# First four attention groups by 64x64 matmuls, the first q and k turned in fp32, 1e-9 as a 65th column, and the issue order of all engines from a table

## The chip, the cores and the metric

The kernel runs on one NeuronCore of one Trainium2 chip. The core has five instruction streams that run side by side and wait for one another by semaphores: TensorE (PE in the profile; its weight loads are a row of their own, PEld), VectorE (DVE), ScalarE (ACT), GpSimd (POOL) and SyncE (SP). Transfers between HBM and the core's memory are issued by POOL, SP and ACT; those of POOL cost POOL time to write their descriptors. Every stream works strictly in the order in which its instructions were written, so an instruction that waits holds up all that stand behind it on its engine.

The metric is the device time of one execution in microseconds (us), as the median of several runs. A lower number is better.

## The reference

```python
def reference(q, k, v, moe_w_in, moe_w_out):          # q, k, v: [8, 8, 576, 64] fp32
    # attention inside chunks of 64 tokens, for each of 8 batches and 8 heads
    q_c, k_c, v_c = (t.reshape(8, 8, 9, 64, 64) for t in (q, k, v))
    scores = (1 / 8) * q_c @ k_c.transpose(0, 1, 2, 4, 3)
    scores = scores - scores.max(-1, keepdims=True)
    attn = exp(scores)
    attn = attn / (attn.sum(-1, keepdims=True) + 1e-09)
    x = (attn @ v_c) -> [4608 tokens, 512]
    h = x @ moe_w_in                                   # [512, 2048]
    g = maximum(0.01 * h, h)
    return g @ moe_w_out                               # [2048, 512] -> [4608, 512] fp32
```

## The kernel before

**Tiling.** The 4608 tokens are 36 groups `u` of 128 tokens (two chunks of 64), and four groups make one of nine blocks `j` of 512 tokens. Attention is done by group. The two linear layers are done by block: block 0 and 1 do the first layer by plain matmuls with a moving side of 128 columns (tasks `L1.j.h.a.p`: block, group within the block, and which 256 columns of `w_in`), the other blocks by seven products in place of eight (`Q1`..`Q7`), and the second layer of all blocks is done by seven products (`P1`..`P7`). PE computes in fp16.

**One attention group** is a chain of tasks; the number behind the dot is the group:

- `loadq`, `loadk`: POOL fetches q and k of the group, fp32 in HBM, fp16 in SBUF. Group 0 comes instead by `q_f` and `k_f` on the queues of SP and ACT, without a conversion, and is cast by `castq`, `castk0`, `castk1`.
- `tq`, `tk`: four PE transposes each (128x128) into PSUM, for groups 0 to 11; for the others a DMA does it.
- `q0`, `q1`: the turned q is copied by ACT or DVE into a tile QZ that is half zeros, each chunk of 64 tokens to its own half of the columns, so that one 128-row matmul computes one head of both chunks. `k`: the same for k in one copy.
- `s`: eight matmuls 128x64 give the scores. `m`, `b`, `x`, `z`: row maximum (DVE), subtraction (DVE), exponential (ACT, fp16 out), row sum (DVE).
- `ze`, `zi`, `n`: add 1e-9 to the sums (DVE or POOL), reciprocal (DVE), scale (DVE or POOL).
- `e`, `c`: PE turns the weights, ACT or DVE copies them; from group 20 a DMA does this instead.
- `v`: eight matmuls with v, 128x64 each, against a tile that has v in two quarters and zeros in the others. `a`: ACT copies the result to xT, the input of the first layer.

For groups 0 to 3 the rows of v come by `v_f` and `loadw`, four copies `put0`..`put3` for each group spread them over a tile (buffers S1 and S2) that four DVE memsets `zg` have zeroed. Later groups use tiles VB that `loadv` fills directly and `zv` has zeroed.

```python
nc.tensor.matmul(                                     # s, before: 8 of these
    out=t["sp"][:, i, :], lhsT=mem(qz)[:, 2 * m + g, e, :, :], rhs=mem(kt)[:, 2 * m + g, e, :],
    start=(i == 0), stop=True, skip_group_check=True)
...
nc.tensor.matmul(                                     # v, before: 8 of these
    out=t["xp"][:, i, e, :], lhsT=vg(u)[:, i, e] if u in VROW else VB[b % NVB][:, i, c, :],
    rhs=mem(et)[:, i // 2, e, i % 2, :], start=(e == 0 and i == 0), stop=True, skip_group_check=True)
```

**Order.** The order of work is not written out. Each piece is a task with an engine (or a choice of engines), an estimated duration, dependencies and the buffers that it holds; `Plan.run` plays them through with its own model of durations and transfers, picks on each engine the ready task with the lowest key, and emits the instructions in the order of the planned starts. The keys are shifted by some 1400 numbers (`NUDGE`) and 36 tasks are moved by hand afterwards (`MOVES`). Where the plan has PE idle in the first 24 us, it puts in matmuls whose result nobody reads (`idle`, 140 in all), after 45 of the same kind at the very start (`warm`).

POOL's loads are bound in one more way: eight transfers may be under way, so a ninth waits for the landing of the one eight places ahead of it. The lines that the profile names for these tasks: L1995 `warm`, L2677 `idle`, L2143 `tq` and `tk`, L2212 `s`, L2218 `m`, L2221 `b`, L2225 `x`, L2237 `z`, L2240 `ze`, L2243 `zi`, L2246 `n`, L2272 `e`, L2290 `v`, L2370 `L1`, L2421 the `Q` products, L2543 the `P` products, L2007 and L2009 all copies on ACT and DVE, L1925 `loadq` and `loadk`, L1940 the loads of `w_in`, L1937 `loadv`, L1986 `ident`.

Of the kernel before, what the change touches and what calls it, by code (L numbers as in the profile page):

```python
# [15 lines left out]
LATENCY = {PE: 0.2, ACT: 0.15, DVE: 0.18, POOL: 0.2, SP: 0.2}  # L16


class Buf:


    def __init__(self, ring):
        self.ring, self.slot, self.open, self.since, self.till = ring, None, 0, 0.0, 0.0


class Task:
    def __init__(self, name, engs, key, emit, deps, bufs, opens, after, bank):
        self.name, self.engs, self.key, self.emit = name, engs, key, emit
        self.eng = next(iter(engs))
        self.deps, self.bufs, self.opens, self.after, self.bank = deps, bufs, opens, after, bank  # L30
        self.next, self.start, self.end, self.seen = [], None, None, None

    @property
    def us(self):
        return self.engs[self.eng]


class Dma:


    LAG = {"soft": 1.7, "hard": 0.5}
    SHARE = {"soft": 0.38, "hard": 0.62}
    SPARE = {"soft": 0.0, "hard": 0.0}

    def __init__(self):
        self.rings = {"soft": [], "hard": []}
        self.now = 0.0
        self.known = None
        self.wide = False

    def add(self, ring, at, work, t):
# [2660 lines left out]
```

## Time and profile before

| | |
|---|---|
| median of 3 runs | 279.45 us (278.21 to 279.82) |
| profiled execution, first to last instruction (span) | 276.6 us |
| what lies around the span, median less span | 2.8 us |
| PE busy | 267.6 us, 97% of the span |
| DVE, ACT, POOL busy | 226.7, 207.9, 139.1 us |

The profile gives one execution, so a sum of its durations is compared with its span, and the 2.8 us around it are taken to stay as they are. PE's busy time counts the unread matmuls `warm` and `idle` as well. Matmuls are pipelined: the one with 128 columns is listed with 219 ns, but eight in a row start some 56 ns apart.

### The profile page before, as it was taken

Reading aid. Unit: us, or ns where it says so; the run is one execution under the profiler, and the core shown is the slowest. Engines: PE = TensorE matmul, PEld = TensorE weight load, DVE = VectorE, ACT = ScalarE, POOL = GpSimd, SP = SyncE. Lnnn points to the kernel's source line nnn. Section 1 sums busy time; section 2 is a strip of 40 time slices with the busy share of each in tenths; the row PEclk is TensorE's granted clock in tenths of the full one; section 3 lists DMA queues with packets and bytes.
Section 4 is the critical chain, followed back from the end, with each engine's and each line's share of the span. In section 5 each row is a group of like instructions: output and inputs, shape, how many; then the busy total and the mean of one; then the engine's idle time right before and its main releaser. Section 6 shows DMA issues by size and latency. Waiting matters only on the chain.

```text
span 276.6 us, 8050 instructions
## 1 busy us (share of the span) xinstructions
PE 267.6 (97%) x3257; PEld 242.9 (88%) x3257; DVE 226.7 (82%) x426; ACT 207.9 (75%) x396; POOL 139.1 (50%) x180
## 2 busy tenths in 40 slices
PE   7888999999999999999999999999999999999995
PEld 7777999999988979898989889889899888988884
DVE  6888899899989899899998999888699927734942
ACT  6878999786786899799877897476877767677431
POOL 8978688567776338244936996562333120000000
PEclk9999999999999999999999999999999999999999
DMA  9999999999999989999999999999543032200132
GB/s 148 162 178 173 166 176 194 139 154 114 149 186 169 190 103 123 113 168 194 136 179 143 154 169 168 211 142 213 113 94 118 19 40 81 76 2 0 68 146 92
DMA packets 157237, 37.09 MB, mean 134 GB/s; under 512 B 147601, under 2 KB 152849, under 8 KB 157201
## 3 DMA queue, kind: packets, MB, share of 16 engines
q0 software_dynamic: 113904, 17.96, 100.9%
q1 hardware_dynamic: 42256, 18.36, 37.7%
q8 instruction: 25, 0.41, 0.7%
q10 hardware_dynamic: 1040, 0.26, 0.4%
q14 instruction: 12, 0.09, 0.1%
HBM read 36.70 MB, written 9.44 MB: 167 GB/s over the span
## 4 chain that ended last, share of the span: by engine, by line
PE 81%; DMA 9%; POOL 5%; ACT 1%; DVE 1%; issue 1%; POOLq 0%
PE bank L2543 38%; PE bank L2421 30%; PE bank L2370 6%; DMA VB<-in_v_dram 4%; DMA w_inT<-in_moe_w_in_dram 3%; PE bank L2290 3%; PE bank L2212 2%; DMA qk<-in_k_dram 2%; POOL qk L1925 2%; PE bank L2272 1%; POOL xs L2093 1%; PE bank L2143 1%; PE bank L2585 1%; DVE xs L2317 1%; ACT ex L2225 0%
## 5 line engine op out<-in xcount | busy, mean ns | idle before, releaser
L2347 ACT ACTIVATE gT<-bank 128x512 f16<-128x512 f32 x116 | 64.9, 600 | 13.9 <-PE bank L2421 12.3
L2543 PEld LDWEIGHTS <-gT 128*128 128x128 f16 x576 | 55.2, 98 | 6.3
L2543 PE MATMUL bank<-w_outT,gT 128*128 128x256 f16 x432 | 53.7, 273 | 0.0
L2421 PEld LDWEIGHTS <-FI 128*128 128x128 f16 x448 | 43.2, 98 | 5.7 <-issue 0.9
L2421 PE MATMUL bank<-xs,FI 128*128 128x256 f16 x336 | 45.8, 272 | 0.4 <-ACT bank L2007 0.3
L2543 PEld LDWEIGHTS <-S 128*128 128x128 f16 x416 | 39.7, 98 | 4.7 <-DVE S L2489 0.3
L1925 POOL DMA_DIRECT2D qk<-in_q_dram x39 | 33.8, 870 | 10.9 <-DMA QT<-qk 4.2
L1925 POOL DMA_DIRECT2D qk<-in_k_dram x39 | 34.0, 878 | 8.6 <-DMA KT<-qk 5.6
L2421 PEld LDWEIGHTS <-w_inT 128*128 128x128 f16 x336 | 32.1, 98 | 3.9 <-issue 0.2
L2543 PE MATMUL bank<-FO,S 128*128 128x256 f16 x280 | 34.8, 273 | 0.0
L2370 PE MATMUL bank<-xT,w_inT 128*128 128x128 f16 x512 | 32.7, 219 | 0.3 <-DMA w_inT<-in_moe_w_in_dram 0.3
L2421 PE MATMUL bank<-xT,w_inT 128*128 128x256 f16 x224 | 31.6, 273 | 0.0
L2370 PEld LDWEIGHTS <-w_inT 128*128 128x128 f16 x512 | 29.4, 98 | 0.5 <-DMA w_inT<-in_moe_w_in_dram 0.5
L2007 ACT ACTIVATE p<-bank 128x512 f32<-128x512 f32 (+1 forms) x37 | 20.6, 588 | 10.0 <-PE bank L2543 5.7
L2246 POOL TENSOR_TENSOR en<-ex,z 128x512 f16<-128x512 f16 x18 | 20.6, 1149 | 14.0 <-DVE z L2243 5.3
L2237 DVE TENSOR_REDUCE z<-ex 128x8 f32<-128x512 f16 x36 | 24.4, 677 | 2.7 <-ACT ex L2225 2.4
L2218 DVE TENSOR_REDUCE mx<-bank 128x8 f32<-128x512 f32 x36 | 24.5, 682 | 1.8 <-PE bank L2212 1.5
L2446 DVE TENSOR_TENSOR bank<-bank,p 128x512 f32<-128x512 f32 x28 | 19.0, 694 | 8.3 <-PE bank L2421 5.9
L2225 ACT ACTIVATE ex<-sh 128x512 f16<-128x512 f32 x35 | 22.2, 634 | 3.0 <-DVE sh L2221 1.5
L2221 DVE TENSOR_TENSOR sh<-bank,mx 128x512 f32<-128x512 f32 x35 | 23.7, 680 | 0.5
L2240 POOL TENSOR_SCALAR z<-z 128x8 f32<-128x8 f32 x25 | 7.5, 301 | 32.7 <-DVE z L2237 26.7
L2007 ACT ACTIVATE xT<-bank 128x512 f16<-128x512 f32 x36 | 21.2, 599 | 3.0 <-PE bank L2290 2.8
(84 smaller groups left out, 479.2 us busy)
## 6 DMA issues: line engine op xcount, KB each, us to landing
out_dram<-osb SPq DMA_DIRECT2D x16, 512.0 KB, 5.2
VB<-in_v_dram POOLq DMA_DIRECT2D x14, 288.0 KB, 7.8
qk<-in_k_dram POOLq DMA_DIRECT2D x31, 128.0 KB, 6.5
qk<-in_q_dram POOLq DMA_DIRECT2D x31, 128.0 KB, 7.9
w_outT<-in_moe_w_out_dram POOLq DMA_DIRECT2D x4, 512.0 KB, 11.0
w_inT<-in_moe_w_in_dram POOLq DMA_DIRECT2D x6, 256.0 KB, 6.9
qk<-in_k_dram POOLq DMA_DIRECT2D x8, 64.0 KB, 7.0
w_inT<-in_moe_w_in_dram POOLq DMA_DIRECT2D x4, 128.0 KB, 6.3
```

Source lines behind the costliest of these rows:

```text
L1925: nc.gpsimd.dma_start(out=to[a - r0:z - r0, which], in_=src[a // S, :, a % S:a % S + z - a, :].rearrange("h p d -> p h d"),)
L2007: nc.scalar.activation(out=to(), in_=of(), func=AFT.Copy, bias=0.0, scale=1.0)
L2218: nc.vector.tensor_reduce(out=mem(mx)[:, 0], in_=t["sp"], axis=AXL.X, op=ALU.max)
L2221: nc.vector.tensor_tensor(out=mem(sh), in0=t["sp"], in1=mem(mx)[:, 0].unsqueeze(2).to_broadcast((128, 8, CH)), op=ALU.subtract)
L2225: nc.scalar.activation(out=mem(ex), in_=mem(sh), func=AFT.Exp, bias=0.0, scale=SCL)
L2237: nc.vector.tensor_reduce(out=mem(z)[:, 0], in_=mem(ex), axis=AXL.X, op=ALU.add)
L2246: (nc.gpsimd if eng == POOL else nc.vector).tensor_tensor(out=mem(en), in0=mem(ex), in1=mem(z)[:, 2].unsqueeze(2).to_broadcast((128, 8, CH ...
L2347: nc.scalar.activation(out=to, in_=of, func=AFT.Prelu, bias=0.0, scale=1.0, alpha=0.01)
L2370: nc.tensor.matmul(out=t["h"][:, i, :], lhsT=w_inT[:, n, fc * 128:(fc + 1) * 128], rhs=xT[:, n, r0 % RING:r0 % RING + tb], start=(i == 0 a ...
L2421: nc.tensor.matmul(out=ps[to][:, i, :], lhsT=lhs[:, t, f:f + 128], rhs=rhs()[:, t], start=(opens and i == 0 and t == 0), stop=(t == 1), sk ...
L2446: nc.vector.tensor_tensor(out=ps["V"], in0=ps["X"], in1=mem(p5), op=ADD)
L2543: nc.tensor.matmul(out=ps[into[m]][:, p - ps_of[0], :], lhsT=lhs[m][0]()[:, fc, p * 128:(p + 1) * 128], rhs=rhs[m][:, fc, :], start=(opens ...
```

## The change

Five edits go together.

1. **Scores of groups 0 to 3 by 64x64 matmuls** (`SROW`). The turned q is copied once, whole (`q0` alone, into QT), and `s` becomes 16 matmuls that each use 64 rows and 64 columns of the array: head by head, chunk by chunk. No zeros are needed.
2. **The product with v of groups 0 to 3 in the same way** (`VROW`). `v` becomes 16 matmuls 64x64 that read the rows of v as they were loaded. The 16 `put` copies and the four `zg` memsets go; one cast `castv` comes in for group 0. The result lies in two PSUM banks, and two copies of half the size, `a0` and `a1`, replace `a`.
3. **Group 0 is turned in fp32.** `castq`, `castk0` and `castk1` go; `tk.0` and `tq.0` transpose q_f and k_f as they landed, against an fp32 copy of the identity (`wide`, a DVE cast of `ident`).
4. **1e-9 as a 65th column**, for all groups. The exponentials lie in fp32 in a tile 128x8x65 whose last column holds 1e-9 (`tiny`, two memsets), so the row sum adds it and all 36 `ze` go. `n` reads fp32 in place of fp16.
5. **The order comes from a table.** The planner, its keys and its moves go; `TABLE` names each task in turn with its engine, its buffers and the unread matmuls (94 of `idle` in place of 140). All engines' orders differ from before throughout. Group 25 is now done as all others (before, its eight heads had an exponential each, on ACT).

```diff
-        "ex": ([128, 8, CH], FP16), "z": ([128, 3, 8], FP32), "en": ([128, 8, CH], FP16),
+        "ex": ([128, 8, CH + 1], FP32), "z": ([128, 2, 8], FP32), "en": ([128, 8, CH], FP16),
...
+    wide_t = task("wide", {DVE: 0.16, ACT: 0.32}, 0, -96.4, lambda eng: move(lambda: wide, lambda: ident)(eng), deps=[ident_t])
+    tiny = [
+        task(f"tiny.{i}", DVE, 0.08, -60.0 + i, lambda i=i: nc.vector.memset(MEM["ex"][i][:, :, CH:CH + 1], 1e-9))
...
             def go():
-                ps[which] = bank((qp, kp)[which], [128, 4, 2, CH], FP16)
+                ps[which] = bank((qp, kp)[which], [128, 4, 2, CH], FP32 if of32 else FP16)
                 for i in range(4):
-                    nc.tensor.transpose(out=ps[which][:, i, :, :], in_=of()[:, 2 * i:2 * i + 2, :], identity=ident)
+                    nc.tensor.transpose(out=ps[which][:, i, :, :], in_=of()[:, 2 * i:2 * i + 2, :], identity=wide if of32 else ident)
...
+            if u in SROW:
+                for i in range(8):
+                    for s in range(2):
+                        part = slice(s * CH, (s + 1) * CH)
+                        o = i if u in VROW else 4 * (i // 2 % 2) + 2 * (i % 2) + i // 4
+                        nc.tensor.matmul(
+                            out=t["sp"][part, o, :], lhsT=mem(qz)[part, i // 2, i % 2, :], rhs=mem(kt)[part, i // 2, i % 2, :],
+                            start=True, stop=True, skip_group_check=True,
+                        )
+                return
...
-        def emit_ze(eng, z=z):
-            (nc.gpsimd if eng == POOL else nc.vector).tensor_scalar_add(out=mem(z)[:, 1], in0=mem(z)[:, 0], scalar1=1e-9)
...
+            if u in VROW:
+                t["xp"] = [bank(x, [128, NT, CH]) for x in xps]
+                w = mem(et).rearrange("p g e s q -> p (g e) s q")
+                for i in range(NT):
+                    for e, m in ((0, 0), (1, 1), (0, 1), (1, 0)):
+                        part, h = slice(e * CH, (e + 1) * CH), 4 * m + i
+                        nc.tensor.matmul(
+                            out=t["xp"][e][m * CH:(m + 1) * CH, i, :], lhsT=row_view(u)[part, h, :], rhs=w[part, h // 2, h % 2, :],
+                            start=True, stop=True, skip_group_check=True,
+                        )
+                return
...
-        vput[u] = [
-            task(
-                f"put{2 * e + m}.{u}", {DVE: 0.27, ACT: 0.43, POOL: 0.42}, 0, key + 40.0, move(
...
+TABLE = """
+k_f:ACT still:DVE q_f:SP zq.0:DVE warm:PE:0 v_f:SP:0 loadQ.2.1:POOL zeros:DVE blank:DVE tiny.0:DVE loadk.2:POOL:0 loadq.2:POOL loadq.1:POOL:1 loadk.1:POOL
+idle:17:2 ident:POOL loadQ.4.0:POOL wide:DVE tk.0:PE:1 loadq.4:POOL:2 tq.0:PE:2 k.0:DVE:0 idle:17:0 q0.0:ACT:0 zq.1:DVE loadq.3:POOL:3 zv.1.0.0:ACT tiny.1:DVE
...
-    for emit in plan.run(filler=(filler, emit_idle), moves=KNOBS.get("MOVES", ())):
-        emit()
+    plan.run(TABLE, idle)
```

**What moves, place one: the start of POOL.** Before, with the waits that each row has:

```order
L1986 AFFINE_SELECT ident<-ident 128x128 [waits DVE_49]
L1925 DMA qk_63<-in_k_dram 128x8x64
L1925 DMA qk_64<-in_q_dram 128x8x64
L1925 DMA qk_65<-in_k_dram 64x8x64 x2
L1925 DMA qk_63<-in_q_dram 128x8x64
```

After, on the same engine:

```order
L289 DMA w_inT<-in_moe_w_in_dram 64x4x512
L274 DMA qk_63<-in_k_dram 128x8x64
L274 DMA qk_63<-in_q_dram 128x8x64
L274 DMA qk_64<-in_q_dram 128x8x64
L274 DMA qk_64<-in_k_dram 128x8x64
L335 ISA
L335 AFFINE_SELECT ident<-ident 128x128 [waits DVE_49,PE_49]
L289 DMA w_inT<-in_moe_w_in_dram 64x4x512
```

The identity is written behind five loads instead of ahead of all of them, and it now waits for PE too: the first 17 `idle` matmuls read the tile `ident` while it is still blank. A piece of `w_in` (`loadQ.2.1`) goes first.

**Place two: DVE in the softmax of the first groups.** Before, from `m.0` on (KT, QZ, QT are turned k and q, mx, sh, ex, z, en the softmax's tiles, et the turned weights):

```order
L2218 TENSOR_REDUCE mx_80<-bank 128x8
L2221 TENSOR_TENSOR sh_82<-bank,mx_80 128x512
L2009 COPY QZ_78<-bank 64x8x64
L2237 TENSOR_REDUCE z_86<-ex_84 128x8
L2240 TENSOR_SCALAR z_86<-z_86 128x8
L2243 RECIPROCAL z_86<-z_86 128x8
L2246 TENSOR_TENSOR en_88<-ex_84,z_86 128x512
L2218 TENSOR_REDUCE mx_81<-bank 128x8
```

After, from `m.0` on:

```order
L560 TENSOR_REDUCE mx_80<-bank 128x8
L563 TENSOR_TENSOR sh_82<-bank,mx_80 128x512
L363 COPY QT_69<-bank 128x512
L363 COPY QT_70<-bank 128x512
L578 TENSOR_REDUCE z_86<-ex_84 128x8
L560 TENSOR_REDUCE mx_81<-bank 128x8
L581 RECIPROCAL z_86<-z_86 128x8
L560 TENSOR_REDUCE mx_80<-bank 128x8
L584 TENSOR_TENSOR en_88<-ex_84,z_86 128x512
L563 TENSOR_TENSOR sh_83<-bank,mx_80 128x512
L563 TENSOR_TENSOR sh_82<-bank,mx_81 128x512
L363 COPY QT_71<-bank 128x512
```

Group 0 no longer goes through alone: the maxima of groups 2 and 1 stand between its row sum and its scaling, and the copies are whole tiles.

**Place three: POOL around the loads of v for groups 4 to 7 (VB) and of `w_out`.** Before:

```order
L1937 DMA VB_115<-in_v_dram 64x36x64
L1937 DMA VB_114<-in_v_dram 64x4x64
L1925 DMA qk_64<-in_q_dram 128x8x64
L1946 DMA w_outT<-in_moe_w_out_dram 128x4x512 x2
L2240 TENSOR_SCALAR z_87<-z_87 128x8
L1925 DMA qk_67<-in_k_dram 128x8x64
```

After:

```order
L286 DMA VB_114<-in_v_dram 64x4x64
L295 DMA w_outT<-in_moe_w_out_dram 128x4x512
L584 TENSOR_TENSOR en_88<-ex_84,z_86 128x512
L584 TENSOR_TENSOR en_89<-ex_85,z_87 128x512
L286 DMA VB_114<-in_v_dram 64x4x64
L274 DMA qk_67<-in_q_dram 64x8x64 x2
L295 DMA w_outT<-in_moe_w_out_dram 128x4x512
```

POOL now does the scaling `n` of groups 7, 4, 5 and 6, between its loads, and 27 of the 36 in all (18 before; DVE did 18 and now does 9). The `ze` rows are gone.

More of the change, by code (lines that the diff above doesn't have):

```diff
@@ L2185, in attention @@
         if u == 0:
[L2186 to L2198 removed]
+            rows[0] = [qf, kf]
+            qz, kt, ready = turn_pe(0, key, [qf], [kf], lambda: q_f, lambda: k_f, [], True)
         elif u in QK_PE:
```

2065 lines of the change are left out of this document (208 added, 1857 removed).

## The prediction

> **What bounds the kernel now.** I read the stretches of the span first, then the unread matmuls `idle` alone in the same stretches.
>
> ```profile
> core 0: us, PE busy (x) PEld busy (x) DVE busy (x) ACT busy (x) POOL busy (x), PEclk, DMA share, GB/s
> 0.00:5.14 5.14, 4.16 (x44) 4.17 (x45) 3.48 (x12) 3.66 (x6) 4.23 (x10) 1.00 0.70 142
> 5.14:20.10 14.96, 12.20 (x214) 10.84 (x212) 11.70 (x25) 11.86 (x24) 13.45 (x19) 1.00 1.94 169
> 20.10:43.65 23.55, 22.19 (x415) 21.20 (x413) 20.93 (x40) 20.86 (x39) 18.60 (x25) 1.00 2.00 174
> 43.65:273.40 229.75, 229.00 (x2594) 206.72 (x2591) 190.33 (x352) 171.48 (x329) 102.80 (x128) 1.00 1.33 128
> ...
> 5.14:20.10 14.96, 8.56 (x130) 7.53 (x130) 1.00 1.94 169
> 20.10:43.65 23.55, 1.05 (x13) 0.62 (x10) 1.00 2.00 174
> ```
>
> In the last stretch PE stands still for 229.75 - 229.00 = 0.75 us of 230. Its matmuls there are the same after the change, so almost nothing can be won behind 43.65 us; a new order can only lose there. Between 20.10 and 43.65 PE waits 23.55 - 22.19 = 1.36 us and spends 1.05 us on `idle`. Ahead of 20.10, where the first layer starts, 8.56 us are `idle`. So a gain must come from reaching the state of 43.65 us earlier. The granted clock is 1.00 in every stretch.
>
> Next the rows of PE that mark this front, in order of time (start, duration, line, form, count, and in brackets the idle time before and what ended it):
>
> ```profile
> 5.20 0.83 PE L2677 MATMUL idle<-ident 128*128 128x128 f16 x12
> 5.87 0.39 PE L2143 MATMUL bank<-ident,qk 128*128 128x128 f16 x4
> ...
> 9.45 0.39 PE L2212 MATMUL bank<-KT,QZ 128*128 128x64 f16 x8
> ...
> 20.10 0.61 PE L2370 MATMUL bank<-xT,w_inT 128*128 128x128 f16 x8
> ...
> 38.88 0.63 PE L2290 MATMUL bank<-et,VB 128*128 128x64 f16 x16
> ...
> 42.66 0.40 PE L2272 MATMUL bank<-ident,en 128*128 128x128 f16 x4 [0.46 <-POOL en L2246]
> ```
>
> These are `idle`, `tq.0`, `s.0`, the first `L1` (20.10), `v.7` with `v.4` (38.88) and `e.5`. And the chain of waits goes, up to 38 us, through loads:
>
> ```profile
> 7.96 6.09 DMA qk<-in_k_dram
> ...
> 15.22 8.17 DMA w_inT<-in_moe_w_in_dram
> ...
> 27.79 10.16 DMA VB<-in_v_dram
> ```
>
> Each row is one load from its issue to its landing: `loadk.1` lands at 14.05, `loadQ.2.1` at 23.39, `loadv.1.0` at 37.95. `v.7` reads that last one. So it is loads that hold the front, and the first question is when `v.7` can run after the change.
>
> **The loads.** I count what each load reads: 256 KB for a group's q, k or v rows and for a narrow piece of `w_in`, 512 for a wide one, 576 for `loadv`. In the order before, 5120 KB are read up to `loadQ.2.1` and 9408 up to `loadv.1.0`: 4288 KB in 14.56 us, 294 KB/us. In the new order 9600 KB are read up to `loadv.1.1`, on which `v.7` waits: 37.95 + 192/294 = 38.6. But POOL starts earlier:
>
> ```profile
> 1.07 0.29 POOL L1986 TENSOR_SCALAR_AFFINE_SELECT ident<-ident 128x128 f16<-128x128 f16 x1 [0.64 <-DVE ident L1983]
> 1.39 1.12 POOL L1925 DMA_DIRECT2D qk<-in_k_dram  x1
> ```
>
> Before, the first load stood behind `ident` (1.39). Now five loads stand ahead of it and can go when the engines are released, at 0.72 (where ACT and SP issue theirs): 0.67 earlier, so `loadv.1.1` lands at 37.9. That `ident` now waits for 17 `idle` matmuls (5.20 + 17 x 0.06 + 0.22, about 6.3 us) costs the loads nothing: the five ahead are 1536 KB, over 4 us of transfers, which cover the stall. The bounds: the two `loadv` follow each other now, and one alone took up to 3.9 us, as the loads before it show:
>
> ```profile
> L1940 POOL DMA_DIRECT2D w_inT<-in_moe_w_in_dram x1: 642/642/642, 27.2 to 27.2; - x1
> ...
> DMA to landing us min/median/max: 6.9/6.9/6.9
> ```
>
> (`loadQ.6.0`: 8832 KB by 34.1; then 576 KB until 37.95.) By its rate 8448 KB, the last load ahead of the two, are there at 32.3; two of 3.9 end at 40.1. The other bound is PE itself, worked out next.
>
> **Part by part: attention of the first groups.** DVE rows give the spacing of starts: maximum to its own subtraction 0.73, subtraction or scaling to the next 0.61, copy 0.33, reciprocal 0.23; an exponential takes 0.63.
>
> ```profile
> 14.70 0.41 DVE L2009 COPY et<-bank 128x512 f16<-128x512 f16 x1
> 15.03 0.68 DVE L2221 TENSOR_TENSOR sh<-bank,mx 128x512 f32<-128x512 f32 x1
> ...
> 20.05 0.69 DVE L2246 TENSOR_TENSOR en<-ex,z 128x512 f16<-128x512 f16 x1
> 20.66 0.20 DVE L2243 RECIPROCAL z<-z 128x8 f32<-128x8 f32 x1
> 20.89 0.69 DVE L2246 TENSOR_TENSOR en<-ex,z 128x512 f16<-128x512 f16 x1
> ...
> 30.16 0.69 DVE L2218 TENSOR_REDUCE mx<-bank 128x8 f32<-128x512 f32 x1
> 30.89 0.69 DVE L2221 TENSOR_TENSOR sh<-bank,mx 128x512 f32<-128x512 f32 x1
> 31.50 0.68 DVE L2218 TENSOR_REDUCE mx<-bank 128x8 f32<-128x512 f32 x1
> ...
> L2225 ACT ACTIVATE ex<-sh 128x512 f16<-128x512 f32 x35 | 22.2, 634 | 3.0 <-DVE sh L2221 1.5 <-DVE z L2240 1.3
> L2237 DVE TENSOR_REDUCE z<-ex 128x8 f32<-128x512 f16 x36 | 24.4, 677 | 2.7 <-ACT ex L2225 2.4
> L2218 DVE TENSOR_REDUCE mx<-bank 128x8 f32<-128x512 f32 x36 | 24.5, 682 | 1.8 <-PE bank L2212 1.5
> L2009 DVE COPY p<-bank 128x512 f32<-128x512 f32 x1 | 0.7, 677 | 0.0
> L2007 ACT ACTIVATE KT<-bank 128x512 f16<-128x512 f16 x11 | 6.5, 591 | 0.3
> L2212 PE MATMUL bank<-KT,QZ 128*128 128x64 f16 x288 | 14.0, 193 | 1.5 <-ACT QZ L2007 0.7 <-DVE QZ L2009 0.7
> ```
>
> - *Turning in fp32.* `ident` ends at 6.3 + 0.3, its cast `wide` is about 0.25, so `tk.0` starts at 6.9, where `tq.0` before started at 5.87: the casts that go (0.5 us) are paid back by the new wait. No row shows an fp32 transpose. An fp16 one starts 57 ns behind the last ((0.39 - 0.22)/3). Between that and four times that I take twice, 0.11: `tk.0` and `tq.0` are issued by 7.8. `q0.0` (0.59) ends at 8.6, `s.0` starts at 9.0 (9.45 before).
> - *64x64 scores and v.* A pack of eight starts 28 ns apart ((0.39 - 0.19)/7); 16 cost 0.45 instead of 0.22, or as before if pairs run side by side. Eight packs are 1.8 us more PE at most. Five of them stand ahead of the first `L1`, where `idle` covers them: 94 there in place of 140.
> - *DVE up to `k.3`*, on which `s.3` and then the first `L1` wait in the new order. `m.0` 9.65, `b` +0.73, two copies, then `z.0` behind its exponential (11.8), `m`, `zi`, `m`, `n.0`, `b`, `b`, copy, `z.1`, `zi`, `z.2`, `n.1`, `zi`, `k.3`: 11.8 + 9 x 0.61 + 0.33 + 3 x 0.23 + 0.41 for `k.3` itself is 18.7. `s.3` follows, and `L1` starts at 19.3 against 20.10.
> - *From there to `v.7` without a wait*: 29 pieces of `L1` at 0.45 ((0.61 - 0.22)/7 = 56 ns a matmul), 8 transposes at 0.23, four `s` at 0.22, three `v` at 0.45 make 17.1: 36.4.
>
> So PE could be at `v.7` at 36.4, but its load is there at 37.9. The 1.5 us between are room: late evictions and drains between packs of other shapes cost nothing until they sum to more. I take 37.9, 0.98 ahead of 38.88. By then PE has done, by the order, one piece of `L1`, one transpose and one `s` more and one `e` less than before: 0.45 + 0.23 + 0.22 - 0.23 = 0.67. The wait of 0.46 at 42.66 goes: `n.5` stands on POOL behind the issue of `loadP.0`, which waits for `loadv.1.1` (37.9), and is done 0.8 + 1.15 later, 39.9; PE is at `e.5` only 2.9 us after `v.7`, 40.8. `v.4` is late next: its chunk is loaded 1664 KB behind `loadv.1.1`, 43.6 at 294 KB/us, and PE is there at 42.9; I take nothing for it, since the wide rows of `w_out` in these 1664 KB should go faster, and keep 0.7 for the range.
>
> - *The 65th column.* An fp16 and an fp32 row operand cost the same in a row sum (677 and 682 ns). 36 `ze` go, 25 on POOL and 11 on DVE, none of which PE waits for behind 43.65: zero. Two `tiny`, `castv` against 16 `put` and four `zg`, the half copies `a0` and `a1`: all ahead of 37.9 in the room above.
> - *The order behind 43.65.* DVE gives up nine `n` (0.68 each) and its `ze`, and takes about as much in copies from ACT; it has 229.75 - 190.33 = 39 us free there, ACT and POOL more. Group 25 takes two instructions in place of its eight exponentials. Between -0.75 (all waits go) and the rivals below; I take zero.
>
> The sum: 0.98 + 0.67 + 0.46 = 2.1 us. The span of 276.6 becomes 274.5, and with the 2.8 us by which the median stands above the profiled span, **277.3 us**.
>
> **The rivals.**
>
> *Fp32 passes.* Speaking for it: no row here has an fp32 matmul. If each needs four passes with four weight loads of its own (98 ns beside 56), the eight take 4.9 us in place of 0.9, `L1` starts at 23.3, PE is at `v.7` at 40.4: 1.5 lost, 0.67 and 0.46 won, 279.8. The Trainium skill, FP8 and Floating Point Precision, TensorE Precision Notes, says that true FP32 makes four passes through the array; by it alone this rival would be right, and no run shown here bears it out yet. Against it: only `tk.0` and `tq.0` are concerned, and 1.5 us of it fall in the room.
>
> *POOL holds DVE (slower).* `n` now reads two fp32 operands, and 27 of them run on POOL. The trace shows one holding the other:
>
> ```profile
> 139.24 1.02 DVE L2618 TENSOR_TENSOR S<-gT,S 128x1024 f16<-128x1024 f16 x1
> ...
> 141.66 1.28 DVE L2618 TENSOR_TENSOR S<-gT,S 128x1024 f16<-128x1024 f16 x1
> ...
> 141.35 1.04 POOL L2246 TENSOR_TENSOR en<-ex,z 128x512 f16<-128x512 f16 x1 [1.63 <-DVE z L2243]
> ...
> 45.00:220.00 175.00, 29.28 (x42) 1.00 1.68 148
> ```
>
> The second DVE sum ends only after POOL's `n` has. The Trainium skill, SBUF — State Buffer, SBUF: two separate sides, has the rule: the two share a port pair as an exclusive lock, whole instructions long; the trace agrees. The last row is DVE's time in such sums, 29.28 of 175 us, 17%. Should `n` double to 2.1 us, 27 of them hold DVE 0.17 x 57 = 9.6 us, against 3.2 for 18 of 1.04: 6.4 more. Half of it reaching PE is 3.2: 280.5. It decides only where `n` gets longer than 2 us; at its present length nothing comes of it.
>
> *Slow loads of v.* Both at 3.9: `v.7` at 40.1, 1.2 lost, 1.1 won: 279.5, no change.
>
> *The old waits go too.* `loadv` in 1.7 us each lets PE reach `v.7` at 36.4, and the 0.75 go: 275.1.
>
> **How the numbers follow.** About 0.5% (1.4 us, below 278.05) is what a measurement of this kernel can tell from no change. The forecast 277.3, with its own range of 276.2 to 278.6, has a chance of 0.55, of which 0.46 lies under 278.05; the old waits going too 0.14; slow loads 0.10 and fp32 passes 0.10, mostly no change; POOL 0.11, slower. Faster: 0.46 + 0.14 + 0.02. No change: 0.09 + 0.15. Slower: 0.11 + 0.03. The range reaches from 275.1 to 280.5.
>
> **What would show it.** `tk.0` at 6.9 and its four transposes 0.11 apart; first `L1` at 19.3; `v.7` at 37.9 with a wait for VB before it; no wait for `en` at `e.5`; POOL's `n` still near 1.1 us; PE standing still under 1.5 us behind that. The forecast is wrong if PE waits for DVE or ACT between 20 and 38 us by more than the room, or if the new order has waits behind 44 us that sum to more than 1 us.

## The result, and the profile after

The changed kernel takes 276.96 us (median of 9 runs, 275.35 to 277.45), the one before 278.21 in the runs beside it. The ratio is 0.9939, with a 95% interval of 0.9917 to 0.9961: faster by 0.6%, close to what this kernel's measurement can tell. (The two medians alone are 0.45% apart, 1.25 us; 0.61% would be 1.7 us.) The prediction was 277.3 us, a gain of 2.1 us on the 279.45 us from which it started. The profiled execution has a span of 274.0 us; over the nine runs the span goes from 273.6 to 275.7 with a median of 274.5, so a single profile is off by up to 1 us on either side, and differences under that are not read from two profiles alone.

First the stretches of the span, cut as before, and below them `idle` (L1021) alone in the second and third:

```profile
core 0: us, PE busy (x) PEld busy (x) DVE busy (x) ACT busy (x) POOL busy (x), PEclk, DMA share, GB/s
0.00:5.14 5.14, 4.13 (x43) 4.14 (x44) 0.77 (x5) 1.28 (x1) 4.09 (x9) 1.00 0.69 141
5.14:20.10 14.96, 12.28 (x236) 10.64 (x234) 10.91 (x24) 7.63 (x15) 12.37 (x18) 1.00 1.96 167
20.10:43.65 23.55, 22.30 (x446) 21.32 (x443) 19.89 (x41) 18.73 (x37) 21.65 (x28) 1.00 1.88 164
43.65:270.80 227.15, 226.23 (x2564) 205.16 (x2560) 197.43 (x356) 159.29 (x298) 105.80 (x117) 1.00 1.35 131
...
5.14:20.10 14.96, 6.24 (x94) 1.00 1.96 167
20.10:43.65 23.55, 0.00 (x0) 1.00 1.88 164
```

Behind 43.65 us PE stands still for 0.92 us (0.75 before), and it has 226.23 us of work left there in place of 229.00. The time was won in front, as forecast. PE stands still as long as before in the whole span (274.0 - 265.0 = 9.0; 276.6 - 267.6 = 9.0). What fell is its busy time, by 2.6 us, as much as the 46 unread matmuls that are gone would take (46 x 57 ns). This is bookkeeping and not a cause, since leaving them out alone would turn them into standing still: work that is read has come forward into their place.

PE's rows at the marks of the prediction (the fp32 transposes, `s.0`, `tq.1`, `tk.1`, `v.0`, `s.3`, the first `L1`, `v.1` and the `L1` behind it, `e.3`, the `L1` that waits for `w_in`, `v.7`, `e.5`):

```profile
7.09 1.09 PE L479 MATMUL bank<-w,u 128*128 128x128 f32 x8 [0.69 <-DVE w L363]
8.02 1.11 PE L1021 MATMUL idle<-ident 128*128 128x128 f16 x17
...
9.49 0.44 PE L547 MATMUL bank<-KT,QT 64*64 64x64 f16 x16
...
11.18 0.40 PE L479 MATMUL bank<-ident,qk 128*128 128x128 f16 x4 [0.40 <-DMA qk<-in_q_dram]
...
12.51 0.40 PE L479 MATMUL bank<-ident,qk 128*128 128x128 f16 x4 [0.60 <-DMA qk<-in_k_dram]
...
17.82 0.32 PE L625 MATMUL bank<-et,S 64*64 64x64 f16 x16 [0.39 <-ACT et L361]
...
19.50 0.44 PE L547 MATMUL bank<-KT,QT 64*64 64x64 f16 x16
19.88 0.62 PE L721 MATMUL bank<-xT,w_inT 128*128 128x128 f16 x8
...
20.84 0.32 PE L625 MATMUL bank<-et,S 64*64 64x64 f16 x16
21.09 0.62 PE L721 MATMUL bank<-xT,w_inT 128*128 128x128 f16 x8
...
27.84 0.39 PE L605 MATMUL bank<-ident,en 128*128 128x128 f16 x4
29.32 1.05 PE L721 MATMUL bank<-xT,w_inT 128*128 128x128 f16 x16 [1.09 <-DMA w_inT<-in_moe_w_in_dram]
...
38.18 0.40 PE L634 MATMUL bank<-et,VB 128*128 128x64 f16 x8
...
41.29 0.40 PE L605 MATMUL bank<-ident,en 128*128 128x128 f16 x4
```

`v.7` and `e.5` have no wait any more. The largest wait behind the first `L1` is a new one: 1.09 us at 29.32 for a piece of `w_in`. The chain of waits has that load too (issue to landing), and POOL's rows show how its loads began:

```profile
6.72 7.37 DMA w_inT<-in_moe_w_in_dram
21.56 7.63 DMA w_inT<-in_moe_w_in_dram
```

```profile
1.27 0.79 POOL L289 DMA_DIRECT2D w_inT<-in_moe_w_in_dram  x1 [0.81 <-POOLq L1038]
...
6.48 0.29 POOL L335 TENSOR_SCALAR_AFFINE_SELECT ident<-ident 128x128 f16<-128x128 f16 x1 [0.89 <-PE idle L1021]
```

DVE's row for `m.2`, with its wait; then `n` on POOL, which the prediction priced, and DVE's time in the sums of the second layer between 45 and 220 us:

```profile
13.32 0.69 DVE L560 TENSOR_REDUCE mx<-bank 128x8 f32<-128x512 f32 x1 [0.53 <-PE bank L547]
...
L584 POOL TENSOR_TENSOR en<-ex,z 128x512 f16<-128x512 f32 x27 | 31.2, 1160 | 49.7 <-DVE z L581 19.9
...
45.00:220.00 175.00, 30.09 (x40) 1.00 1.68 147
```

### The profile page after: what moved, and what is told of

Read it like the earlier page. It is cut to its first block, busy times and chain, and to the rows that moved or that the text cites. A ratio compares the mean times of both kernels' runs of the same rounds, so it can differ in the third digit from the quotient of the medians.

```text
span 274.0 us, 8039 instructions
## 1 busy us (share of the span) xinstructions
PE 265.0 (97%) x3275; PEld 241.3 (88%) x3275; DVE 229.2 (84%) x424; ACT 186.9 (68%) x348; POOL 143.9 (53%) x168
## 4 chain that ended last, share of the span: by engine, by line
PE 81%; DMA 8%; POOL 4%; DVE 2%; ACT 2%; issue 1%; POOLq 0%
PE bank L894 36%; PE bank L772 27%; PE bank L721 9%; DMA w_inT<-in_moe_w_in_dram 5%; DMA QT<-qk 3%; PE bank L554 2%; POOL qk L274 2%; PE bank L634 2%; PE bank L349 2%; PE bank L605 1%; ACT gT L698 1%; DVE xs L668 1%; PE bank L479 1%; ACT xT L361 1%; POOL S L436 1%
## 5 line engine op out<-in xcount | busy, mean ns | idle before, releaser
L698 ACT ACTIVATE gT<-bank 128x512 f16<-128x512 f32 x116 | 66.0, 596 | 26.4 <-PE bank L772 21.9
L584 POOL TENSOR_TENSOR en<-ex,z 128x512 f16<-128x512 f32 x27 | 31.2, 1160 | 49.7 <-DVE z L581 19.9
L772 PE MATMUL bank<-xs,FI 128*128 128x256 f16 x336 | 47.1, 273 | 0.0
L772 PE MATMUL bank<-xT,w_inT 128*128 128x256 f16 x224 | 32.3, 273 | 0.0
L567 ACT ACTIVATE ex<-sh 128x512 f32<-128x512 f32 x36 | 22.7, 630 | 9.5 <-DVE sh L563 5.4
L578 DVE TENSOR_REDUCE z<-ex 128x8 f32<-128x520 f32 x36 | 24.5, 683 | 4.0 <-ACT ex L567 3.9
L800 DVE TENSOR_TENSOR w<-bank,p 128x512 f32<-128x512 f32 x28 | 19.0, 680 | 6.2 <-PE bank L772 6.0
L361 ACT ACTIVATE p<-bank 128x512 f32<-128x512 f32 (+1 forms) x29 | 16.7, 580 | 9.1 <-PE bank L894 5.3
L286 POOL DMA_DIRECT2D VB<-in_v_dram x16 | 17.7, 1110 | 7.5 <-PE bank L634 5.7
L361 ACT ACTIVATE xT<-bank 128x512 f16<-128x512 f32 (+1 forms) x33 | 17.7, 563 | 5.2 <-PE bank L634 4.1
```

Of the source, the lines that this page charges most:

```text
L361: nc.scalar.activation(out=to(), in_=of(), func=AFT.Copy, bias=0.0, scale=1.0)
L567: nc.scalar.activation(out=mem(ex)[:, :, :CH], in_=mem(sh), func=AFT.Exp, bias=0.0, scale=SCL)
L578: nc.vector.tensor_reduce(out=mem(z)[:, 0], in_=mem(ex), axis=AXL.X, op=ALU.add)
L584: (nc.gpsimd if eng == POOL else nc.vector).tensor_tensor(out=mem(en), in0=mem(ex)[:, :, :CH], in1=mem(z)[:, 1].unsqueeze(2).to_broadcast( ...
L698: nc.scalar.activation(out=to, in_=of, func=AFT.Prelu, bias=0.0, scale=1.0, alpha=0.01)
L772: nc.tensor.matmul(out=ps[to][:, i, :], lhsT=lhs[:, t, f:f + 128], rhs=rhs()[:, t], start=(opens and i == 0 and t == 0), stop=(t == 1), sk ...
```

## The experiments

Two theories were set against each other. *Loads*: the transfers hold PE up to about 30 us, so work ahead of them is free. *Chain*: the attention of the first groups holds the first layer, and each edit counts one to one. Each ratio is taken to the kernel before, on the same chip; its interval is the 95% one. The changed kernel's is 0.9939 (0.9917 to 0.9961). The medians of the kernel before beside these runs go from 278.2 to 278.6 us, so medians of different rows are comparable to some 0.4 us only. Each profile shows one execution, and often not a typical one: e1's took 276.78 us, e5's 276.32, e6's 276.08 and e10's 278.13. Its rows tell what that execution waited for, not where a difference of medians lies.

| kernel | median us | ratio | interval |
|---|---|---|---|
| e1: group 0 cast first, turned in fp16 | 275.62 | 0.9895 | 0.9863 to 0.9926 |
| e2: `ze` and fp16 back | 277.65 | 0.9985 | 0.9967 to 1.0004 |
| e3: padded scores back | 276.89 | 0.9940 | 0.9924 to 0.9957 |
| e4: padded v and `put` back | 277.45 | 0.9966 | 0.9950 to 0.9983 |
| e5: identity first | 275.34 | 0.9883 | 0.9854 to 0.9911 |
| e6: one load more | 277.64 | 0.9962 | 0.9934 to 0.9990 |
| e7: `loadq.5` behind `w_in` | 278.42 | 0.9994 | 0.9967 to 1.0022 |
| e8: e5 and e1 | 275.46 | 0.9892 | 0.9836 to 0.9948 |
| e9: e5, no standing ahead of `tk.2` | 275.33 | 0.9877 | 0.9822 to 0.9933 |
| e10: e5, 30 `idle` ahead of `tk.0` | 275.99 | 0.9911 | 0.9884 to 0.9938 |
| e11: e9, `loadw.1` earlier | 275.53 | 0.9888 | 0.9856 to 0.9921 |
| e12: fp16, 1e-9 left out | 275.53 | 0.9895 | 0.9875 to 0.9915 |

**One edit undone at a time: e1 to e4.** All are the changed kernel with its table, and the tasks of the edit put back into it.

e1, the fp32 turning undone:

```diff
-            qz, kt, ready = turn_pe(0, key, [qf], [kf], lambda: q_f, lambda: k_f, [], True)
+            ck = task("castk", {DVE: 0.46, ACT: 0.5}, 0, -59, move(lambda: half(1), lambda: k_f), deps=[kf])
+            cq = task("castq", {DVE: 0.46, ACT: 0.5}, 0, -60, move(lambda: half(0), lambda: q_f), deps=[qf])
+            qz, kt, ready = turn_pe(0, key, [cq], [ck], lambda: half(0), lambda: half(1), [])
...
-idle:17:2 ident:POOL loadQ.4.0:POOL wide:DVE tk.0:PE:1
+idle:17:2 ident:POOL loadQ.4.0:POOL castk:DVE castq:ACT tk.0:PE:1
```

> Edit 3 undone in the changed kernel: castq (ACT) and castk (DVE) turn q_f and k_f into fp16 first, tk.0 and tq.0 are fp16 transposes against ident, wide is gone. Two theories of what holds the front of the changed kernel. Loads: the piece of w_in that lands at 29.18 and for which PE stands 1.09 us at 29.32 sets the course, so whatever shifts the work ahead of it by less than 1.09 us is free; then nothing changes in time (277.0, within 0.4), and the wait at 29.3 only gets longer by what the front gains. Chain: group 0's chain up to the first L1 (19.88) counts one to one; tk.0 starts about 0.2 earlier (ident ends at 6.77 and no cast follows) and eight transposes at 57 ns in place of 117 ns save 0.5 more, so 276.3 and the first L1 at 19.2.

275.62 us, 1.3 less than with the edit; the intervals just touch (0.9926 and 0.9917), so the size is uncertain. As placed, the fp32 turning is no gain and probably a loss. The row shows both parts of the edit, a shorter wait (0.42 in place of 0.69) and the transposes in half the time, but in this execution they start later than in the changed kernel (7.41 against 7.09) and its span is 274.9 us, so it doesn't show the gain itself:

```profile
7.41 0.61 PE L485 MATMUL bank<-ident,FO 128*128 128x128 f16 x8 [0.42 <-POOL ident L342]
```

e2, the additions back:

```diff
-        "ex": ([128, 8, CH + 1], FP32), "z": ([128, 2, 8], FP32)
+        "ex": ([128, 8, CH], FP16), "z": ([128, 3, 8], FP32)
...
+        def emit_ze(eng, z=z):
+            (nc.gpsimd if eng == POOL else nc.vector).tensor_scalar_add(out=mem(z)[:, 1], in0=mem(z)[:, 0], scalar1=1e-9)
```

> Edit 4 undone in the changed kernel: exponentials in fp16 in a tile 128x8x64, 36 additions ze of 1e-9 (16 on DVE, groups 0 to 11 among them, 20 on POOL), n reads fp16. The prediction costed this edit at zero: then 277.0 within 0.4, with 36 additions back and n on POOL at its 1.15 us as before. Rival: the additions stand in DVE's chain of the first groups (four of some 0.15 us up to the first L1) and POOL's additions delay its loads and n; then 0.6 us slower from the front alone (277.6), more with waits for en behind 44 us.

277.65 us, and the interval lies just above the changed kernel's: in this order, the edit is worth about 0.5%, where the prediction had zero. It isn't quite the old state that is back, since 16 of the 36 `ze` stand on DVE here and 11 did before the change. PE's waits in its profile, and below them a row of e5, which has no `ze`:

```profile
22.34 0.32 PE L635 MATMUL bank<-et,S 64*64 64x64 f16 x16 [1.57 <-DMA S<-in_v_dram]
...
78.28 2.79 PE L904 MATMUL bank<-FO,S 128*128 128x256 f16 x24 [1.04 <-DVE S L850]
```

```profile
76.85 2.79 PE L901 MATMUL bank<-FO,S 128*128 128x256 f16 x24 [0.82 <-ACT VB L382]
```

The second wait is DVE's: a sum comes 1.04 us late at 78 us, where the changed kernel has no wait. So DVE has no free time to cover with at that place. But the same matmul waits for 0.82 us in e5's profile and in e3's, which have no `ze`, so this wait can't be put down to them alone. The first wait is a load and changes from one execution to the next (e9, e10).

e3, the padded scores back (zeroed tiles in a part of `FO`, which nothing else uses before 51 us):

```diff
- 'SROW': [0, 1, 2, 3]}
+ 'SROW': []}
...
-q0.0:ACT:0
+q0.0:ACT:2 q1.0:DVE
```

> Edit 1 undone in the changed kernel: scores of groups 0 to 3 by eight matmuls 128x64 against tiles that are half zeros, two copies q0 and q1 of each turned q, four more memsets zq on DVE in its idle time before 6.8 us. Loads theory: no change (277.0 within 0.4), the extra copies eat some of the 1.09 us wait at 29.3. Chain theory: q1.0 (0.4 us on DVE) delays s.0 and m.0, three more copies of 0.6 us on ACT delay x.0 to x.2; 0.4 to 1.0 slower (277.4 to 278.0).

276.89 us, no change: edit 1 by itself is worth nothing that these runs show in this order. PE's stretches in its profile show something else:

```profile
11.00:14.00 3.00, 1.13 (x21) 0.76 (x19) 2.02 (x6) 2.56 (x5) 1.51 (x2) 1.00 2.13 165
14.00:17.50 3.50, 3.50 (x40) 3.50 (x40) 2.54 (x5) 1.57 (x3) 3.34 (x5) 0.51 2.00 172
```

`s.1` waited 1.48 us for a copy, PE was busy for 1.13 of 3 us, and then the granted clock was 0.51 for 3.5 us. The mean clock was 0.991 to 0.994 in five of its six runs (0.999 or 1.00 in eight of the changed kernel's nine).

e4, v padded again:

```diff
-castv:ACT:0
+put0.0:ACT put3.0:ACT put1.0:DVE put2.0:DVE
...
-a1.0:ACT
...
-a0.0:ACT
+a.0:ACT
```

> Edit 2 undone in the changed kernel: the product with v of groups 0 to 3 by eight matmuls 128x64 against a half zero tile, 16 copies put (8 on ACT, 8 on DVE) and four memsets zg back, castv gone, one copy a in place of a0 and a1. The rows of v of group 1 land at 20.8, so v.1 now waits for two copies behind that (about 0.5 to 0.9 us more than before on PE). Loads theory: all of it stands ahead of the 1.09 us wait at 29.3 and is covered: 277.0 within 0.5. Chain theory: 8 x 0.27 us more on DVE and 8 x 0.43 on ACT in the stretch up to 24 us make the first layer later by 1 to 2 us: 278 to 279.

277.45 us, 0.5 more, with intervals that overlap (0.9950 and 0.9961): edit 2 probably helps, by about 0.3%. The copies come behind the loads of the rows, and PE waits for them at `v.1`, `v.2` and `v.3`; it also waits for DVE at `e.0`, for 1.15 us:

```profile
22.31 0.73 PE L659 MATMUL bank<-et,S 128*128 128x64 f16 x8 [0.86 <-ACT S L369]
26.49 0.73 PE L659 MATMUL bank<-et,S 128*128 128x64 f16 x8 [0.53 <-ACT S L369]
34.36 0.53 PE L659 MATMUL bank<-et,S 128*128 128x64 f16 x8 [0.87 <-DVE S L371]
```

**Chain or loads: e5, e6, e7, e10.** e5 takes the identity out of the way of both:

```diff
-k_f:ACT still:DVE q_f:SP zq.0:DVE warm:PE:0 v_f:SP:0 loadQ.2.1:POOL zeros:DVE blank:DVE tiny.0:DVE loadk.2:POOL:0 loadq.2:POOL
-loadq.1:POOL:1 loadk.1:POOL idle:17:2 ident:POOL loadQ.4.0:POOL wide:DVE tk.0:PE:1
+k_f:ACT still:DVE blank:DVE q_f:SP zq.0:DVE warm:PE:0 v_f:SP:0 ident:POOL loadQ.2.1:POOL zeros:DVE wide:DVE tiny.0:DVE loadk.2:POOL:0 loadq.2:POOL
+loadq.1:POOL:1 loadk.1:POOL idle:2:2 loadQ.4.0:POOL tk.0:PE:1
```

> The changed kernel with ident written on POOL ahead of the five loads, as before the change, so that it waits for no idle matmul; 2 idle in place of 17 ahead of tk.0. Then tk.0 can start when k_f has landed (5.4) and the cast wide is done, 5.6 in place of 7.09, and POOL does not stand at ident (0.89 us in the changed kernel). Chain theory: s.0, m.0 and all of group 0 come 1.4 us earlier and with them the first L1: about 1 us faster, 276.0. Loads theory: s.2 waits for q2 (11.1) and k1 (12.5), s.3 for k3 (18.2), the first layer for the piece of w_in at 29.2; POOL reaches its ninth load earlier but the transfers are the limit, so within 0.4 of 277.0, the first L1 still near 19.9, and a longer wait in front.

275.34 us, clearly faster than the changed kernel (the intervals are apart), and more than the chain theory had asked for. The rows of the profiled execution tell of loads:

```profile
5.57 1.07 PE L486 MATMUL bank<-w,u 128*128 128x128 f32 x8 [0.30 <-DMA u<-in_k_dram]
...
8.97 0.40 PE L486 MATMUL bank<-ident,qk 128*128 128x128 f16 x4 [1.38 <-DMA qk<-in_k_dram]
...
19.32 0.62 PE L728 MATMUL bank<-xT,w_inT 128*128 128x128 f16 x8
...
27.70 0.39 PE L612 MATMUL bank<-ident,en 128*128 128x128 f16 x4
28.05 1.05 PE L728 MATMUL bank<-xT,w_inT 128*128 128x128 f16 x16
```

`tk.0` is 1.52 us earlier and the first `L1` 0.56, yet `e.3` at 27.70 is only 0.14 ahead of the changed kernel's 27.84: waits for transfers in between have taken the rest. The step is right behind it, 28.05 against 29.32, since the piece of `w_in` has landed in time. This execution is also the one of e5's four in which the clock fell (0.992 as a mean, 0.999 to 1.00 in the others), and its span of 274.5 us is no shorter than the changed kernel's 274.0. So where the gain of the median comes from, its rows don't show.

> The identity first as in e5, but 30 idle ahead of tk.0, so that tk.0 starts at about 7.0 as in the changed kernel (7.09) and only POOL's loads profit. e5 changed two things at once; this parts them. If e5's 1.6 us came through the loads (POOL no longer stops behind its fifth load until the idle matmuls are done), they stay: 275.4. If they came through group 0's chain (tk.0 at 5.57), they go: 276.9. Half and half would be 276.1.

```diff
-idle:2:2 loadQ.4.0:POOL tk.0:PE:1
+idle:30:2 loadQ.4.0:POOL tk.0:PE:1
```

e10 is e5 with `tk.0` held back: 275.99, the "half and half" of the expectation (276.1). Its interval overlaps both neighbours', so nothing is settled. In its profile `tk.0` is held back further than was meant, to 7.98 against 7.09 in the changed kernel, among others because the `warm` matmuls took 4.98 us in place of 4.45. That the median is still not above the changed kernel's speaks for a share of the loads; its size stays open.

e6 puts one more load ahead of the two pieces of `w_in`:

```diff
-loadQ.6.1:POOL
+more:POOL loadQ.6.1:POOL
```

> The changed kernel with one more load of 256 KB (rows of k into a tile that nobody reads by then) on POOL, directly ahead of the two loads of w_in that land at 26.99 and 29.18. Nothing up to the first L1 (19.88) is touched. Loads theory: these two and all behind them land 256/294 = 0.87 us later (and POOL is busy 0.9 us more), PE stands about 2.0 us for w_in in place of 1.09, and the time grows by 0.9: 277.9. Chain theory: what PE does between 20 and 43 us is set by DVE, ACT and PE itself and the wait is only a place where slack shows; then under 0.3 more: 277.2.

277.64 us, 0.7 more: nearer to the 0.9 of the loads theory, with overlapping intervals. Its profile doesn't bear out that theory's mechanism: PE stands 0.85 us for `w_in`, less than the 1.09 in the changed kernel, where 2.0 had been expected. A wait for POOL's `n.5` appears instead. Below PE's two rows are those of POOL and DVE for it:

```profile
28.91 1.05 PE L730 MATMUL bank<-xT,w_inT 128*128 128x128 f16 x16 [0.85 <-DMA w_inT<-in_moe_w_in_dram]
42.13 0.40 PE L614 MATMUL bank<-ident,en 128*128 128x128 f16 x4 [1.28 <-POOL en L593]
...
39.99 2.08 POOL L593 TENSOR_TENSOR en<-ex,z 128x512 f16<-128x512 f32 x1
39.96 1.21 DVE L677 TENSOR_TENSOR FI<-FI,w_inT 128x2048 f16<-128x2048 f16 x1
```

`n.5` starts at 39.99, earlier than in the changed kernel (40.15), but takes 2.08 us in place of 1.08: a sum on DVE (into `FI`) had begun 0.03 us ahead of it. In the changed kernel `n.5` came first, and the same sum took 1.95 us in place of 1.21. So here it is the prediction's rival, one of POOL and DVE holding the other, that reaches PE, and not the extra load as such. This execution is one of the faster of the ten; where the median's 0.7 us comes from stays open.

e7 takes a load away from there:

```diff
-loadq.5:POOL
 loadQ.6.1:POOL
...
 loadQ.6.0:POOL
+loadq.5:POOL
```

> The changed kernel with loadq.5 moved behind the two loads of w_in that PE waits for, and tq.5, s.5 and m.5 moved behind five pieces of L1 to match. The w_in piece then lands some 0.87 us earlier (28.3). Loads theory: the 1.09 us wait at 29.3 shrinks to 0.2; v.7 could be reached at 37.3 but its load lands at 37.7, so some 0.4 us comes back there: 0.4 to 0.9 faster, 276.1 to 276.6. Chain theory: softmax of groups 4 to 7 on DVE limits e.7, e.4, e.5 behind 36 us, and b.5 now comes later: no gain, or a new wait for en at e.5 of up to 1 us: 277.0 to 278.0.

278.42 us, 1.5 slower, intervals apart. The wait for `w_in` went, and in the profile PE waits in its place for a copy of q of group 6 and for `n.5`; a third wait, for a late sum of the first layer at 137 us, is far behind the edit (0.18 us in e6's profile) and may be chance:

```profile
33.60 0.41 PE L561 MATMUL bank<-KT,QZ 128*128 128x64 f16 x8 [0.61 <-DVE QZ L370]
42.26 0.40 PE L612 MATMUL bank<-ident,en 128*128 128x128 f16 x4 [0.20 <-POOL en L591]
...
137.17 1.03 PE L779 MATMUL bank<-xs,FI 128*128 128x256 f16 x8 [0.80 <-DVE bank L804]
```

So the pure loads theory falls for this edit: taking away one transfer's wait by delaying another gained nothing. The chain theory's 277.0 to 278.0 is passed as well.

**From e5 on: e8, e9, e11.**

> The identity first on POOL as in e5, and in addition the fp32 turning undone as in e1 (castk on DVE, castq on ACT, fp16 transposes). This prices the fp32 turning where ident is no longer behind idle matmuls: tk.0 can start behind castk at 5.9 in place of 5.6, its eight transposes take 0.46 in place of 0.93. If e1 won because the fp32 passes cost PE and DVE time on the chain, 0.5 us are won again: 274.9. If e1 won because without wide the wait for ident was shorter, nothing is left to win: 275.3, within 0.4 of e5, since PE waits 1.4 us for k2 (8.97) behind tq.0 either way.

e8 is e5 with e1's edit: 275.46, the same as e5, though four runs leave an interval of 0.56% to either side. So no cost of the fp32 turning is seen where `ident` is not behind `idle`; PE waits for k2 behind it either way (1.38 us in e5, 1.28 here). That e1 won by the shorter wait and not by the number format fits this and is not shown.

> The identity first as in e5, with 33 idle in place of 17 behind tq.0, so that PE does not stand 1.38 us ahead of tk.2, and z.14 on DVE behind S2.1.0, for which PE stood 0.82 us at 76.85 in e5. In e5 the granted clock fell to 0.50 from about 11 to 14.2 us, 2 us behind that stand; a run with 1.48 us of standing at 12.4 to 13.9 showed the same from 14 to 17.5. If standing causes the fall, the clock stays 1.00 here, s.2, s.1 and 29 idle matmuls between 11 and 15 go at full speed, e.0 starts some 0.5 us earlier than 15.09, and with the 0.8 us of the second edit the time is 274.0 to 274.8. If the fall has another cause, the clock falls again and only the second edit counts: 274.6 to 275.2. If the waits are only moved along, 275.3.

```diff
-idle:17:0 q0.0:ACT:0
+idle:33:0 q0.0:ACT:0
...
-z.14:DVE:0 tq.19:SP:0 cp1.1.0:ACT:0 P4.0.p1:PE S2.1.0:DVE
+tq.19:SP:0 cp1.1.0:ACT:0 P4.0.p1:PE S2.1.0:DVE z.14:DVE:0
```

275.33, no change against e5. Both waits are gone, and the clock held, as it did by the mean clock (0.999 to 1.00) in three of e5's four runs without the filling: this doesn't show that standing still caused the fall. First e5's stretch, then e9's, and the wait that came instead:

```profile
7.50:9.00 1.50, 0.12 (x3) 0.04 (x2) 0.00 (x0) 0.91 (x2) 0.91 (x2) 1.00 2.41 155
...
10.90:14.20 3.30, 3.18 (x54) 2.73 (x52) 3.17 (x8) 2.31 (x4) 2.67 (x4) 0.51 2.11 168
```

```profile
10.90:14.20 3.30, 2.88 (x65) 2.48 (x65) 3.27 (x8) 2.31 (x4) 2.55 (x4) 1.00 2.10 168
...
21.80 0.32 PE L632 MATMUL bank<-et,S 64*64 64x64 f16 x16 [1.50 <-DMA S<-in_v_dram]
```

The last row is `v.1`, for rows of v that landed at 21.75 (20.23 in e5's execution, with the same list of loads ahead of it). e11 moves that load:

```diff
-loadk.6:POOL:0
...
 loadw.1:POOL
+loadk.6:POOL:0
```

> As e9 (identity first, 33 idle behind tq.0, z.14 behind S2.1.0), with the rows of v of group 1 (loadw.1) one load earlier, ahead of loadk.6, and tk.6 later on PE, ahead of tk.4. In the profiles so far that load lands anywhere from 20.23 to 22.30 us, and PE stands up to 1.57 us for it at v.1 (1.50 in e9, 1.37 in e10), right behind the first L1. If this stand is what kept e9 at 275.3 in spite of two waits removed, it goes with a landing about 0.9 us earlier and the median is 274.2 to 274.8. If the loads as a whole hold PE until 29 us, the next load (k6, w_in or v rows of group 2) is waited for in its place: 275.3 within 0.4.

275.53 us: no gain over e9 that the runs show, though between 20.10 and 43.65 PE hardly stands still any more:

```profile
20.10:43.65 23.55, 23.41 (x467) 22.43 (x465) 20.61 (x41) 19.78 (x39) 22.49 (x28) 1.00 1.90 170
```

The first `L1` of that execution starts later (19.82 against 19.46 in e9), so little is left to win between 20 and 44. The lead does last in the profiles: PE's last matmul ends at 270.05 us, against 270.75 in e9 and 270.64 in the changed kernel. But the span goes on for 4.15 us behind it, 3.75 in e9 and 3.36 in the changed kernel, and that takes the lead back. With the medians of six and four runs, from 274.2 to 277.3 us, 0.7 us can't be told.

**e12: what the 65th column costs.** 1e-9 is left out, by e2's edit without `ze`.

> The changed kernel with exponentials in fp16 in a tile 128x8x64 and 1e-9 left out altogether: no ze, no 65th column. e2, which had the 36 ze and fp16, took 277.65 against 276.96. If the ze were what cost there, this kernel is at 277.0 or, if the fp32 operand and the 65th column have a price of their own, below (276.5). If e2 lost for another reason, such as the fp16 writing by ACT or the chance of load landings (PE stood 1.9 us for rows of v in its profile), this one stays at 277.6.

275.53 us, and the interval is below the changed kernel's. Against e2, which differs by the 36 `ze` alone, they cost 2.1 us by the medians in this order. Against the changed kernel the 65th column would cost 1.4, and that no instruction shows: `z`, `x` and `n` take 676, 629 and 1190 ns here and 683, 630 and 1160 there. In its profile the piece of `w_in` is there in time (the `L1` of 29.32 starts at 28.05). Whether fp16 has to do with that, or only this execution, stays open.

The versions with the identity first (e5, e8, e9, e11) all lie at 275.3 to 275.5 us, 0.5% below the changed kernel and 1.2% below the one before; e5 is the smallest edit among them. But e1 and e12, which leave the identity where the change puts it, reach 275.6 and 275.5, so its place isn't shown to be what holds the changed kernel. What the new order alone brings, without the four other edits, was not tried: that the order is the main cause of the gain is argued here and not shown. Undoing the four one at a time changes the ratio by -0.44, +0.46, +0.01 and +0.27%, together 0.3 of the 0.6%; whether they add up is not known.

## Why the prediction was right, point by point

- *The gain lies in front, nothing behind 43.65.* Right: standing still went from 0.75 to 0.92 us there, and 2.77 us less of work was left, against a sum of 2.1. The predicted span of 274.5 is the median of the nine. The 2.8 us around the span did not stay as they were: over the nine runs they go from 1.75 to 3.05.
- *POOL's loads start 0.67 earlier.* Wrong: 1.27 against 1.39, 0.12. POOL has a wait of 0.81 of its own ahead of its first load, which `ident` had filled before. `loadv.1.1` still landed at 37.69 (37.9 forecast), so this term's error was made up elsewhere, in loads that came faster than the sum had them.
- *`ident` behind 17 `idle` costs nothing.* `ident` started at 6.48 (6.3 forecast), after a stall of 0.89 us. That the place costs nothing is refuted for its two effects together, the late loads and the late `tk.0`, by e5 (1.6 us); which of them it is stays open.
- *`tk.0` at 6.9, transposes 0.11 apart.* 7.09, and eight in 0.93 us, 0.116 each, twice the fp16 ones. The rival of four passes was wrong. The Trainium skill, FP8 and Floating Point Precision, TensorE Precision Notes, has four passes for true FP32; the measured spacing of these transposes doesn't bear it out, and the measurement decides.
- *First `L1` at 19.3.* 19.88. Two steps failed. `s.0` came at 9.49 in place of 9.0, behind a late `tk.0`, 17 `idle` and `tk.2`, and with it `z.0` at 12.09 in place of 11.8. And the count from `m.0` to `k.3` had no loads in it: PE waited 0.40 for q1 and 0.60 for k1, `s.2` stands behind them, and DVE waited 0.53 us for it at `m.2`. The rest of the count was 0.2 too long. Of the 0.8 us that were to be won on 20.10, 0.6 were lost here.
- *`v.7` at 37.9, held by its load.* 38.18, held by nothing. The "room" of 1.5 us was used up by that late start and by the 1.09 us for `w_in` at 29.32, a load that I had not followed; so it is this load, and not `loadv.1.1`, that held the front in this execution. The work between was sized rightly: 18.30 us from the first `L1` to `v.7`, less the wait, are 17.2, and 17.1 were forecast. The term of 0.98 measured 0.70; the work done ahead of `v.7` (0.67) and the wait of 0.46 at `e.5`, which is gone, are as forecast. That makes 1.8 of the 2.6 us by which this profile is shorter; the rest is not traced to a term.
- *64x64 packs cost 0.45 where padded ones cost 0.22.* Too dear. The `L1` behind `v.1` starts 0.25 us after it, the one behind `s.3` 0.38, and the padded `v.7` takes 0.23 (38.18 to the next row of PE at 38.41). e3 and e4 show no loss by them.
- *The 65th column is worth zero.* As a step from the kernel before this stands: PE waited for no `ze` behind 43.65 there. The reason was wrong: in the new order the `ze` would cost 0.7 us (e2, 277.65). I had set DVE's free 39 us of 230 against them; that is a mean over stages, and in e2's profile DVE has no wait from 66 to 79 us.
- *POOL holds DVE.* `n` stayed at 1160 ns (under the 2 us from which it decides), so the rival was rightly small. It is there: a sum takes 752 ns (30.09/40) in place of 697 (29.28/42) with 27 `n` on POOL in place of 18, but PE waits for none of them in this execution. In e6's it waits 1.28 us for an `n` that a DVE sum holds, so the rival is there with the roles exchanged.

So what was right is where the gain lies and its size in the span: 2.1 us forecast, 2.6 in the profile. The mechanism was right in part, and some of the agreement is luck. The start of the loads was overrated and a load was forgotten, while the loads came faster and the packs were cheaper than the sum had them. And the kernel before ran at 278.21 us in the runs beside the changed one, 1.2 us less than the 279.45 from which the forecast started: the time was met within 0.4 us, with a gain of 1.25 us by the medians in place of 2.1.

## What to carry to other kernels

Where engines fill their waits with work that nobody reads, count that work before and after: its decrease equals the gain in the profile here, while the sum of the waits didn't move. Follow every load whose reader is on the path, not only the one that ended the last wait; and be wary of an instruction on the engine that issues the loads that waits for filler on another engine (moving it ahead won 0.5% here, by which of its effects is open). Free time of an engine, averaged over a span, says nothing of one stretch: look at the one in which the extra instruction falls. And don't explain a difference of medians by the profile of one execution without looking where that execution lies among the runs.

## What the runs showed of the hardware

In two profiles the granted clock fell to 0.51 after PE had stood still: in e5 after 1.38 us of standing that ended at 8.97, from 10.9 to 14.2 us, and in e3 after 1.48 us that ended at 13.90, from 14.0 to 17.5 us. In the 3.4 us ahead of the fall PE was busy for 1.86 us in e5 and for 1.53 in e3. It doesn't always follow: in e1's profile PE stood for 2.0 us, was busy for 1.27 of the 3.4 us from 14.0 to 17.4, and the clock stayed at 1.00.

```profile
15.00:17.00 2.00, 0.03 (x1) 0.00 (x0) 0.78 (x2) 1.75 (x3) 0.87 (x2) 1.00 2.19 162
17.00:20.00 3.00, 2.88 (x58) 2.56 (x59) 2.50 (x7) 0.66 (x2) 2.60 (x4) 1.00 2.03 173
```

The Trainium skill, TensorE: Matmul & The Clock Gate, Part 1: The HAM clock gate, has half rate after an idle window of about 3.4 us that runs freely. The falls of 3.3 and 3.5 us are about as long as one such window. That a fall can follow a standing still of under half a window is what these rows add; what decides between e1 and the others they don't show.

The 45 `warm` matmuls at the start take from 4.01 to 4.98 us, by the execution (e3 and e1 here), and whatever waits for PE early, as `ident` did, inherits that spread:

```profile
1.00 4.01 PE L357 MATMUL bank<-still 128*128 128x128 f16 x45 [1.00 <-DVE still L359]
```

```profile
1.00 4.98 PE L355 MATMUL bank<-still 128*128 128x128 f16 x45 [1.00 <-DVE still L357]
```

The piece of `w_in` for which PE waited at 29.32 landed between 27.91 (e5, e12) and 29.81 us (e4) in these profiles, among kernels with the same loads up to there. And from the end of PE's last matmul to the end of the span it took 3.3 us (e8) to 4.3 us (e10). Differences smaller than such spreads can't be read from two profiles.
